# A second level of Strassen for product 4 of the output (g22 by w_out's fourth sum), with its quarters in attention's PSUM banks

## The chip, the cores and the metric

The kernel runs on one core of one Trainium2 chip. The metric is the device time of the whole kernel in microseconds (us), inputs and outputs in the chip's memory; lower is better. All data are float32.

The engines are named as the profile names them: PE (TensorE, matrix products), PEld (its loading of weights, beside the products), DVE (VectorE), ACT (ScalarE), POOL (GpSimd) and SP (SyncE, which here issues most transfers). TensorE writes its results to PSUM, [...] and VectorE and ScalarE empty them.

## The reference

```python
# attention without softmax, per batch b (8) and head h (8), seq 576, head_dim 64
kv  = np.einsum('bhsd,bhse->bhde', k, v)
out = np.einsum('bhsd,bhde->bhse', q, kv)
rms = np.sqrt(np.mean(out * out, axis=-1, keepdims=True) + 1e-06)
out = out / rms * g_norm
# then two layers on 4608 tokens of 512: w_in is 512 x 2048, w_out 2048 x 512
x = out.transpose(0, 2, 1, 3).reshape(4608, 512)
h = x @ w_in
g = np.maximum(0.01 * h, h)
return g @ w_out
```

Nearly all of the work is in the two large products, x @ w_in and g @ w_out.

## The kernel before

The 4608 tokens are worked in nine blocks of 512 (i = 0 to 8). The hidden units are worked in four groups (c = 0 to 3). A pair (block, group), from block 1 on, is a round, numbered n = (i - 1) * 4 + c, 0 to 31. Block 0 is computed without Strassen, at the start.

**Products by Strassen.** Each large product of a round is split into 2 x 2 quarters and computed as seven products of quarters rather than eight (the Winograd form). The products are numbered 1 to 7. Products 1, 6, 7 and 4 accumulate one after the other in one PSUM bank, products 2 or 5 and 3 in another; after each, the bank's running sum is added to the quarters of the output that need it:

```python
def strassen(tags, left, right, done, order=ORDER, pieces=None):
    banks = {}
    for i in order:
        if i is None:
            yield
            continue
        b = tags[0 if i in (1, 6, 7, 4) else 1]
        if i in FRESH:                              # FRESH = (1, 2, 5)
            banks[b] = ps_m.tile([P, 2, N2], F32, tag=b, name=f"{b[0]}_{b[1]}")
        bank = banks[b]
        ...
        for part in range(2):
            for r in range(2):                      # four matmuls of 128 x 256
                matmul(bank[:, part, :], lhsT=left(i, part, r), rhs=right(i, part, r),
                       start=i in FRESH and part == 0 and r == 0, stop=(r == 1), ...)
        done(i, bank.rearrange("p u (v n) -> p (u v) n", v=2))
        yield
```

**The hidden product (h), by two levels.** From block 2 on, each of the seven products of x @ w_in is again computed by seven, all as matmuls of 128 x 128. A round has seven h groups, in the order 1, 2, 6, 5, 7, 3, 4. Each h group has seven such matmuls and, where `second` is set, an eighth: it fills the fourth quarter of bank h_hb or h_hd with a matmul of product 2 of the output of an earlier round (g12 by w_out), which is by two levels too. The sums that make g from the seven, and the leaky ReLU, follow the seventh group:

```python
def product_h_two(i, c, quarters, to, second):
    ...
    for t, k in enumerate(ORDER):                   # ORDER = (1, 2, 6, 5, 7, 3, 4)
        for js, tags, q in zip(GROUPS, (("ha", "hc"), ("hb", "hd")), (qa, qc)):
            ...                                     # four matmuls in ha or hc, three in hb or hd
            if len(js) < 4 and second:
                second.product(k, banks[tag][:, 3, :])
            ...
            if fresh:
                nc.scalar.copy(q[:, at], bank)
            else:
                add(nc.vector, q[:, at], bank, q[:, at])
            if len(js) < 4 and second:
                second.done(k, banks[tag][:, 3, :])   # a 128 x 128 add into the output
        read(n0 + t + 1 + RING)                     # w_in's next operand, from memory
        yield
    g11, g21, g22, g12 = g_of(c)
    add(nc.vector, g21, qa[:, :, 0, :], qa[:, :, 1, :])
    add(nc.vector, g11, qa[:, :, 0, :], qc[:, :, 0, :])
    yield
    ...                                             # five more sums
    for t in (g11, g12, g22, g21):
        relu(t)                                     # ScalarE
    sums_of(c, to)                                  # GpSimd: the sums of g that Strassen needs
```

**The output product (o).** It follows two slots behind h. A slot holds one h group and then one o group; a round has seven slots. In rounds n = 4 to 29 product 2 is left to the h groups, and the order of the o groups is 1, 5, 6, none, 7, 3, 4. The banks are oa and oc; from one round to the next they change places:

```python
def product_o(n, g_sides, os, finish, second):
    w_sides, _ = sides_w2(n)
    sums = sides_w2(n + 1)[1] if n + 1 < NC * (NB - 1) else lambda i: None
    ...
    into = {1: ("11", True), 5: ("22", True), 2: ("11", False), 6: ("12", True),
            3: ("12", False), 7: ("22", False), 4: ("21", True)}

    def done(i, bank):
        key, fresh = into[i]
        ...
        if c == 0 and fresh:
            nc.scalar.copy(to, bank)
        else:
            add(nc.vector, to, bank, to)            # 128 x 512
        ...
        if i == (6 if second else 5):
            sums(0)                                 # the next round's sums of w_out, t12
        elif i == 4:
            sums(1)                                 # and t34: from memory, on SyncE's queue

    yield from strassen((("oa", "oc"), ("oc", "oa"))[n % 2], ...,
                        (1, 5, 6, None, 7, 3, 4) if second else ORDER, pieces=pieces)
```

**Attention** for the next block runs beside these, in pieces, at fixed slots (`FINE_SLOTS`, `LATE_SLOTS`). It has two PSUM banks of its own; the other six are ha, hb, hc, hd, oa and oc:

```python
ps_att = ctx.enter_context(tc.tile_pool(name="ps_att", bufs=2, space=PSUM))   # tag "att"
ps_m   = ctx.enter_context(tc.tile_pool(name="ps_m", bufs=1, space=PSUM))
...
FINE_SLOTS = {1: 1, 2: 1, 4: 1, 9: 1, 10: 2, 11: 1, 12: 1, 15: 1, 16: 2, 17: 2, 18: 1, 19: 1,
              23: 1, 24: 1, 25: 1, 26: 1}           # slot in the block (7 * c + t): steps
HELD = (22, 24, 26)                                 # slots without an o group in the last block

def both_outputs(b, lo, hi, sums, kv=None):
    tiles = att_tiles("o_ps")                       # both banks
    ...                                             # matmuls 64 x 32, then:
    for l in range(2):
        nc.scalar.activation(sq, o_ps[l], func=AF.Square)
    for l in range(2):
        for e in range(2):
            nc.scalar.activation(x[:, 2 * l + e, :], o_ps[l][:, e, :], func=AF.Copy, ...)
```

A slot's order, with what it emits: the h group; the attention's steps of this slot, x's sums for the next block (VectorE at slots 20 to 22, GpSimd at 24 and 25) and the transfers; `inner_g` (four GpSimd sums of g for product 2's second level, two at the fifth slot of a round and two at the seventh); at last the o group. From block 2 on each engine works in the order in which the program emits.

Of the kernel before, what the change touches and what calls it, by code (L numbers as in the profile page):

```python
# [23 lines left out]
def kernel(  # L24
# [39 lines left out]
    P = 128  # L64
# [34 lines left out]
    NW = U * NE * P  # L99
    w1_all = consts.tile([P, 2 * NC * NW], F32, name="w1_all")  # L100
    stage = consts.tile([P, 3 * NW], F32, name="stage")
    pairs = consts.tile([P, 4 * NW], F32, name="pairs")
    g_all = [consts.tile([P, 4 * U * N2], F32, name=f"g_{i}") for i in range(2)]

    def view(t, lo, *shape):
        n = 1
        for d in shape:
            n *= d
        t = t[:, lo:lo + n]
        names = "abcd"[:len(shape)]  # L110
        return t.rearrange(f"p ({' '.join(names)}) -> p {' '.join(names)}",
                           **dict(zip(names, shape))) if len(shape) > 1 else t

    def pair(i, *shape):
        return view(pairs, i * NW, *shape)

    def matmul(*args, **kw):
        pin(nc.tensor.matmul(*args, **kw))  # L118
# [66 lines left out]
    zeros = view(g_all[0], 0, NT)  # L185
    nc.vector.memset(zeros[:, :64], 0.0)
    nc.vector.memset(zeros[:, 64:], 0.0)
    ident = consts.tile([P, P], F32, name="ident")

    def make_ident():  # L190
        pin(nc.gpsimd.memset(ident, 1.0))
# [449 lines left out]
    def sides_w1(c):  # L641
# [9 lines left out]
        def more():  # L651
# [5 lines left out]

    w2_dram = [[dram.tile([P, 2, U, N2], F32, name=f"w2_{c}_{i}") for i in range(2)]
               for c in range(NC)]
    t12, t34 = pair(2, 2, U, N2), pair(3, 2, U, N2)  # L660
    writes = []

    def sides_w2(n):

        c = n % NC
        b11, b12 = w2_sb[0][c][:, :, :N2], w2_sb[0][c][:, :, N2:]
        b21, b22 = w2_sb[1][c][:, :, :N2], w2_sb[1][c][:, :, N2:]

        def sums(i):
            t = (t12, t34)[i]
            if n >= NC:
                pin(nc.sync.dma_start(t, w2_dram[c][i]))
                return
            if i == 0:
                add(nc.gpsimd, t[:, 0], b12, b11, True)
                add(nc.gpsimd, t[:, 1], b22, t[:, 0], True)
            else:
                add(nc.gpsimd, t[:, 0], b22, b12, True)  # L680
                add(nc.gpsimd, t[:, 1], b21, t12[:, 1], True)
            if (n, i) == (NC - 1, 1):

                writes.append((w2_dram[c][i], t))
            else:
                pin(nc.sync.dma_start(w2_dram[c][i], t))
        return {1: b11, 2: b21, 3: b22, 5: t12[:, 0], 6: t12[:, 1], 7: t34[:, 0],
                4: t34[:, 1]}, sums
# [49 lines left out]
    def read(to):  # L738
        nonlocal n_read
        while n_read < min(to, len(reads)):  # L740
# [5 lines left out]
    qc = pair(0, 4, 3, P)  # L746
    xt1 = [work.tile([P, 2, N2], F32, tag="xt1", name="xt1"),
           view(w1_all, RING * NG + 24 * P, 2, N2)]
    xt24 = [work.tile([P, 2, 2, N2], F32, tag="xt24", name="xt24"),
            view(w1_all, RING * NG + 16 * P, 2, 2, N2)]  # L750
    xi = view(stage, 0, 3, 7, P)

# [82 lines left out]
    def g_of(c):  # L835


        return [view(g_all[c % 2], 0, 4, 4, P)[:, :, i, :] for i in range(4)]
# [40 lines left out]

    gi = view(pairs, 12 * P, 4, P)

    def inner_w2(c):
        y = w2_sb[1][c]
# [7 lines left out]

    def inner_g(c, half):

        g = g_of(c)[3]
        a11, a21, a12, a22 = (g[:, n, :] for n in range(4))
        s1, s2, s3, s4 = (gi[:, n, :] for n in range(4))
        if half == 0:
            add(nc.gpsimd, s1, a21, a22)  # L900
            add(nc.gpsimd, s2, s1, a11, True)
        else:
            add(nc.gpsimd, s3, a11, a21, True)
            add(nc.gpsimd, s4, a12, s2, True)

    class Second:
# [17 lines left out]
        def done(self, k, bank):  # L924
            v, s = INTO[k]
            to = self.o[:, v, s * P:s * P + P]
            add(nc.vector, to, bank, to)
            if self.n % NC == NC - 1 and k == ORDER[-1]:
                self.finish("11", self.o)

    def product_h_two(i, c, quarters, to, second):

# [41 lines left out]
    def product_o(n, g_sides, os, finish, second):  # L974

        c = n % NC
        w_sides, _ = sides_w2(n)
        sums = sides_w2(n + 1)[1] if n + 1 < NC * (NB - 1) else lambda i: None
        if c == 0:

            for key in ("12", "22", "11", "21"):
                os[key] = opool.tile([P, 2, N2], F32, tag="o", name=f"o{key}", bufs=6)


        pieces = ((0, slice(0, N2)), (1, slice(0, P)), (1, slice(P, N2))) \
            if n + 1 == NC * (NB - 1) else None
# [5 lines that stand above are left out]
            if isinstance(bank, list):  # L992
                for at, (end, (part, cols)) in enumerate(zip(bank, pieces)):
                    to = os[key][:, part, cols]
                    add(nc.vector, to, end, to)
                    if i == ORDER[-1]:
                        finish(key, os[key], part, cols, (nc.sync, nc.scalar)[at % 2])
                if i == 7:
                    finish(key, os[key])
                return  # L1000
            to = os[key].rearrange("p u (v n) -> p (u v) n", v=2)
# [3 lines that stand above are left out]
                add(nc.vector, to, bank, to)  # L1005
            if c == NC - 1 and i in (2, 7, 3, 4):
                finish(key, os[key])

            if i == (6 if second else 5):
                sums(0)  # L1010
            elif i == 4:
                sums(1)


        yield from strassen((("oa", "oc"), ("oc", "oa"))[n % 2], lambda i, part, r: g_sides[i][:, 2 * r + part, :],
                            lambda i, part, r: w_sides[i][:, r, :], done,
                           (1, 5, 6, None, 7, 3, 4) if second else ORDER,
                           pieces=pieces)
# [100 lines left out]
    HELD = (22, 24, 26)  # L1119
    o_queue, waited = collections.deque(), 0  # L1120

    seconds = {}

    def second_of(n):
        if n in seconds:
# [9 lines left out]
    for i in range(1, NB):  # L1135
# [4 lines left out]
        for c in range(NC):  # L1140
# [3 lines left out]
            for t in range(7):  # L1144
                slot = 7 * c + t
                go(h_steps, 1)
                if not one:

                    if t == 6:
                        go(h_steps, 1)  # L1150
                    if slot in LATE_SLOTS:
                        go(late, 1)
                    for _ in range(FINE_SLOTS.get(slot, 0)):
                        go(a_steps, 1)
                    if i + 1 < NB:
                        if slot == 20:
                            x_sides, new_quarters, sums, inner = sides_x(i + 1)
                        if slot in (20, 21, 22):
                            go(sums, 2 if slot == 20 else 1)
                        if slot == 24:  # L1160
                            inner(0)
                        elif slot == 25:
                            inner(1)
                    load_some()

                now = (i - 1) * NC + c
                if now - 1 in seconds:
                    for half in range(2):
                        if t == (6 if half else 4):
                            inner_g((now - 1) % NC, half)  # L1170
                    if t == 5 and now <= 2 * NC:
                        inner_w2((now - 1) % NC)
                if slot == 4 and not one:
                    while writes:
                        pin(nc.sync.dma_start(*writes.pop()))
                if slot in HELD and i == NB - 1:
                    pass
                elif waited == LAG:
                    go_o()
                elif o_queue:  # L1180
                    waited += 1
                if one:

                    if t == 1:
                        combine(c, 2)
                    if t == 3 and c < NC - 1:
                        h_sides, more_h = sides_w1(c + 1)
                        combine(c + 1, 0)
                    if t == 5 and c < NC - 1:
                        more_h()  # L1190
                        combine(c + 1, 1)
                    if slot == 5:
                        in_line = True
                        go(late, 1)
                        in_line = False
                    if slot in A_SLOTS:
                        go(a_steps, 1)
                    load_some()
                    if slot == 24:
                        go(a_steps)  # L1200
                        x_sides, new_quarters, sums, inner = sides_x(i + 1)
                        go(sums)
                    elif slot == 25:
                        inner(0)
                    elif slot == 26:
                        inner(1)
# [47 lines left out]
```

## Time and profile before

| | |
|---|---|
| time, median of 3 runs | 918.29 us (917.94 to 919.58) |
| span of the profiled run | 916.1 us |
| PE busy | 909.3 us, 99% |
| DVE busy | 631.6 us, 69% |
| POOL busy | 370.2 us, 40% |
| ACT busy | 328.2 us, 36% |
| moved by DMA | 200.05 MB, mean 218 GB/s |
| 128 x 512 add of a bank of oc into the output, DVE | 684 ns |
| 128 x 128 add of the fourth quarter of hb into the output, DVE | 287 ns |
| 128 x 128 sum of g, POOL | 459 ns |

The profile comes from one execution. The page gives busy times by engine, then groups of instructions with count and mean time of one; other views give the waits by engine, and all instructions in order of time. In these lines out<-in are the names of the tiles written and read, L118 is the line of the helper through which all matmuls go, and L637 the one of the helper for additions and subtractions. A float32 matmul is recorded as two instructions. The lengths of matmuls are modelled and overlap; the time that one takes up is read from where the next one starts.

### The profile page before, as it was taken

The page shows a single profiled execution, that of the slowest core. Times are in us where ns is not written, and L with a number is a line of the kernel's source. Part 1 is how long each engine was busy: PE and PEld are TensorE (multiplying, and loading weights), DVE is VectorE, ACT ScalarE, POOL GpSimd, SP SyncE. Part 2 cuts the span into 40 slices and gives each one's busy share as a digit, 9 for nine tenths or more (in the row PEclk, how much of TensorE's full clock was granted, in tenths as well). Part 3 has the DMA queues.
Part 4 walks back from the last instruction along what each step waited for, and adds up shares of the span by engine and source line. Part 5 has one row for each costly group of instructions (what it writes and reads, how often), then busy time and mean ns, then how long its engine had stood idle before and what let it go on. Part 6 is the DMA issues. An engine that isn't in the chain of part 4 may idle for free.

```text
span 916.1 us, 18037 instructions
## 1 busy us (share of the span) xinstructions
PE 909.3 (99%) x6980; PEld 776.3 (85%) x6980; DVE 631.6 (69%) x1168; ACT 328.2 (36%) x645; POOL 370.2 (40%) x438
## 2 busy tenths in 40 slices
PE   9999999999999999999999999999999999999998
PEld 5444448888998999899999999999999999999997
DVE  4876995587457876587756786678659755755565
ACT  5454533242135233533343324332343333223330
POOL 2000355967633473226421642264226422642222
DMA  8999926885599778776886789658765676667632
GB/s 269 236 245 249 248 85 191 280 285 167 166 360 289 228 209 268 233 230 214 255 247 230 219 249 272 222 178 212 242 183 176 187 222 198 185 185 223 197 109 92
DMA packets 90228, 200.05 MB, mean 218 GB/s; under 512 B 9888, under 2 KB 42272, under 8 KB 90144
## 3 DMA queue, kind: packets, MB, share of 16 engines
q1 hardware_dynamic: 79680, 187.04, 68.6%
q10 hardware_dynamic: 10016, 10.69, 3.4%
q8 instruction: 55, 0.90, 0.4%
q0 software_dynamic: 448, 1.18, 0.3%
q14 instruction: 29, 0.24, 0.1%
HBM read 172.39 MB, written 26.48 MB: 217 GB/s over the span
## 4 chain that ended last, share of the span: by engine, by line
PE 96%; DMA 2%; DVE 1%; issue 0%; ACT 0%; POOL 0%; SPq 0%; ACTq 0%; DVEq 0%; POOLq 0%
PE o_a L118 19%; PE o_c L118 18%; PE h_ha L118 11%; PE h_hb L118 11%; PE h_hc L118 8%; PE h_hd L118 8%; PE o_acc L118 6%; PE h_ps L118 6%; PE o_ps L118 3%; PE h_a L118 2%; PE h_b L118 1%; PE h_c L118 1%; PE h_d L118 1%; PE kv_ps L118 1%; DMA pairs<-in_v_dram 1%; DMA v_in<-in_v_dram 1%
## 5 line engine op out<-in xcount | busy, mean ns | idle before, releaser
L637 POOL TENSOR_TENSOR gs<-g 128x512 f32<-128x512 f32 x64 | 81.7, 1277 | 253.3 <-ACT g L833 253.3
L833 ACT ACTIVATE g<-g 128x512 f32<-128x512 f32 x124 | 78.2, 631 | 131.9 <-DVE g L637 131.9
L952 ACT COPY w_all<-h_ha 128x512 f32<-128x512 f32 x84 | 48.9, 582 | 173.5 <-PE h_ha L118 167.8
L118 PE MATMUL o_a<-pairs,gs 128*128 128x256 f32 x384 | 91.3, 381 | 0.0
L118 PE MATMUL o_c<-pairs,gs 128*128 128x256 f32 x376 | 89.2, 380 | 0.0
L637 DVE TENSOR_TENSOR o<-h_hb,o 128x128 f32<-128x128 f32 x104 | 29.8, 287 | 83.8 <-ACT pairs L952 83.7
L637 DVE TENSOR_TENSOR o<-o_c,o 128x512 f32<-128x512 f32 (+1 forms) x91 | 61.2, 672 | 23.9 <-PE o_c L118 23.6
L118 PEld LDWEIGHTS o_a<-pairs,gs 128*128 128x128 f32 x384 | 69.8, 190 | 9.2 <-POOL pairs L637 1.2
L118 PEld LDWEIGHTS o_c<-pairs,gs 128*128 128x128 f32 x376 | 68.3, 190 | 7.6
L637 DVE TENSOR_TENSOR o<-o_a,o 128x512 f32<-128x512 f32 x75 | 51.2, 683 | 28.2 <-PE o_a L118 28.1
L637 POOL TENSOR_TENSOR pairs<-w_all 128x512 f32<-128x512 f32 x8 | 11.1, 1384 | 120.6 <-ACT cut L245 102.3
L118 PE MATMUL h_ha<-stage,w_all 128*128 128x128 f32 x448 | 59.6, 276 | 0.0
L118 PEld LDWEIGHTS h_ha<-stage,w_all 128*128 128x128 f32 x448 | 56.6, 192 | 3.0 <-issue 0.7
L118 PE MATMUL h_ps<-xT,w_all 128*128 128x512 f32 (+1 forms) x136 | 58.0, 570 | 0.9 <-DVE w_all L258 0.9
L118 PE MATMUL o_acc<-w,g 128*128 128x512 f32 x128 | 57.8, 595 | 0.0
L637 DVE TENSOR_TENSOR g<-g,pairs 128x512 f32<-128x512 f32 x84 | 55.7, 689 | 1.9
L637 POOL TENSOR_TENSOR pairs<-g 128x128 f32<-128x128 f32 x52 | 23.9, 459 | 75.4 <-PE h_hb L118 46.7
L118 PEld LDWEIGHTS h_ps<-xT,w_all 128*128 128x128 f32 x136 | 25.5, 190 | 30.0 <-issue 26.6
L637 DVE TENSOR_TENSOR w_all<-h_hc,w_all 128x512 f32<-128x512 f32 x56 | 38.3, 684 | 15.9 <-PE h_hc L118 15.8
L118 PEld LDWEIGHTS o_acc<-w,g 128*128 128x128 f32 x128 | 24.0, 190 | 29.8 <-issue 29.4
L637 DVE TENSOR_TENSOR o<-h_hd,o 128x128 f32<-128x128 f32 x78 | 22.1, 283 | 37.8 <-ACT pairs L952 37.7
L118 PE MATMUL h_hb<-stage,w_all 128*128 128x128 f32 x336 | 46.7, 275 | 0.0
(228 smaller groups left out, 2264.6 us busy)
## 6 DMA issues: line engine op xcount, KB each, us to landing
w_all<-w SPq DMA_DIRECT2D x196, 448.0 KB, 4.2
pairs<-w SPq DMA_DIRECT2D x56, 512.0 KB, 4.3
out_dram<-o ACTq DMA_DIRECT2D x35, 256.0 KB, 4.6
v_in<-in_v_dram SPq DMA_DIRECT2D x29, 288.0 KB, 5.7
k_in<-in_k_dram SPq DMA_DIRECT2D x28, 288.0 KB, 5.1
q_in<-in_q_dram SPq DMA_DIRECT2D x56, 144.0 KB, 6.0
q_in<-in_q_dram SPq DMA_DIRECT2D x56, 140.0 KB, 5.8
w<-stage SPq DMA_DIRECT2D x12, 512.0 KB, 4.6
```

What stands on the lines that cost most here:

```text
L118: pin(nc.tensor.matmul(*args, **kw))
L637: ins = eng.tensor_tensor(out_, a, b_, op=ALU.subtract if minus else ALU.add)
L833: nc.scalar.activation(t, t if src is None else src, func=AF.Prelu, alpha=SLOPE)
L952: nc.scalar.copy(q[:, at], bank)
```

## The change

Product 4 of the output multiplies g22 by a sum of w_out's quarters. In rounds n = 8 to 29 (blocks 3 to 8) it is no longer four matmuls of 128 x 256 but, by a second level of Strassen, seven of 128 x 128 (quarter products, here q1 to q7). This needs:

- seven operands from w_out (`f4` and `f4_more`): GpSimd makes the three sums and the fourth once per group (`inner_w4`, rounds 4 to 7), they are written to memory, and each later round reads them back;
- four sums of g22: `inner_g` makes them together with those for product 2, 128 x 256 in place of 128 x 128;
- two banks: those of attention. q1, q6, q7 and q4 accumulate in one, q2 and then q5 and q3 in the other. They stand between the groups of the output product: q1 and q2 in the slot that had no o group, q6 and q5 before o7, q7 and q3 after it, q4 in the slot that had o3; o3 moves into the slot that had o4;
- seven additions of 128 x 128 into g21's part of the output, in place of one of 128 x 512. And since product 4 no longer accumulates on products 1, 6 and 7, their running sum is added to that part by an addition of its own (`third`).

The identity matrix moves into a tile that is used later for x's sums, which makes room for the second set of g's sums. Cut to its core:

```diff
+    f4 = t34[:, 1].rearrange("p u (v n) -> p (u v) n", v=2)
+    f4_more = view(stage, 21 * P, 3, P)
+    def four(n):
+        return 2 * NC <= n < NC * (NB - 1) - 2
...
+            if four(n) and i:
+                pin(nc.sync.dma_start(t[:, 0], w2_dram[c][i][:, 0]))
+                pin(nc.sync.dma_start(f4, w4_dram[c][:, :4, :]))
+                pin(nc.sync.dma_start(f4_more, w4_dram[c][:, 4:, :]))
+                return
...
-        g = g_of(c)[3]
-        a11, a21, a12, a22 = (g[:, n, :] for n in range(4))
-        s1, s2, s3, s4 = (gi[:, n, :] for n in range(4))
+        g = view(g_all[c % 2], 0, 4, 4, P)
+        a11, a21, a12, a22 = (g[:, n, 2:, :] for n in range(4))
+        s1, s2, s3, s4 = (gi_two[:, :, n * P:n * P + P] for n in range(4))
...
+    class Fourth:
+        BEFORE = {3: (1, 2), 4: (6, 5), 5: (4,)}
+        AFTER = {4: (7, 3)}
+        ...
+        def some(self, which):
+            for k in which:
+                if k == 1:
+                    self.banks = [ps_att.tile([P, P], F32, tag="att", name="f_ps")
+                                  for _ in range(2)]
+                bank = self.banks[0 if k in (1, 6, 7, 4) else 1]
+                matmul(bank, lhsT=self.left[k], rhs=self.right[k], start=k in FRESH, stop=True,
+                       skip_group_check=True)
+                v, s = INTO[k]
+                to = self.os["21"][:, v, s * P:s * P + P]
+                if self.n % NC == 0 and k in (1, 6, 5):
+                    nc.scalar.copy(to, bank)
+                else:
+                    add(nc.vector, to, bank, to)
+        def third(self, bank):
+            to = self.os["21"].rearrange("p u (v n) -> p (u v) n", v=2)
+            if self.n % NC:
+                add(nc.vector, to, bank, to)
+                return
+            nc.scalar.copy(to[:, 2, :], bank[:, 2, :])
+            add(nc.vector, to[:, :2, :], bank[:, :2, :], to[:, :2, :])
+            add(nc.vector, to[:, 3, :], bank[:, 3, :], to[:, 3, :])
+        def beside(self, steps, last):
+            for j in range(7):
+                self.some(self.BEFORE.get(j, ()))
+                if j == 5:
+                    last()                          # sums(1): the next round's operands
+                next(steps)
+                self.some(self.AFTER.get(j, ()))
+                yield
...
+            if fourth and i == 7:
+                fourth.third(bank)
...
+        if four(n):
+            fourth = Fourth(n, os)
+            yield from fourth.beside(strassen(..., (1, 5, 6, None, 7, None, 3)), last)
+            return
```

## The prediction

> **What bounds the kernel now.** I read the busy times first, then the waits, then the chain that ended last.
>
> ```profile
> PE 909.3 (99%) x6980; PEld 776.3 (85%) x6980; DVE 631.6 (69%) x1168; ACT 328.2 (36%) x645; POOL 370.2 (40%) x438
> ...
> PE 96%; DMA 2%; DVE 1%; issue 0%; ACT 0%; POOL 0%; SPq 0%; ACTq 0%; DVEq 0%; POOLq 0%
> ```
>
> TensorE is busy 99% of the span, and 96% of the chain that ended last is TensorE. The list of waits has four entries for it, 3.4 us in all, none of them in the seven blocks that use the hidden product by two levels. So every microsecond of matmuls saved is a microsecond won, and every microsecond that TensorE is made to wait is lost in full. VectorE has 31% free on average, but it works in order, and its work comes in bursts. I therefore looked at one round (from the last h group of hidden group c = 0 in block 8 to the next round) in order of time, TensorE first:
>
> ```profile
> 823.27 1.06 PE L118 MATMUL h_ha<-stage,w_all 128*128 128x128 f32 x8
> ...
> 825.06 1.89 PE L118 MATMUL o_c<-pairs,gs 128*128 128x256 f32 x8
> 826.79 0.39 PE L118 MATMUL h_ha<-xT,w_all 128*128 128x128 f32 x2
> ...
> 828.57 1.89 PE L118 MATMUL o_a<-w,gs 128*128 128x256 f32 x8
> 830.30 0.38 PE L118 MATMUL h_hc<-xT,w_all 128*128 128x128 f32 x2
> ...
> 832.09 1.89 PE L118 MATMUL o_c<-pairs,g 128*128 128x256 f32 x8
> 833.82 1.05 PE L118 MATMUL h_ha<-stage,w_all 128*128 128x128 f32 x8
> ...
> 835.60 1.03 PE L118 MATMUL o_a<-w,g 128*128 128x256 f32 x4
> ```
>
> Columns: start, length, engine, line, operation, out<-in, count. An fp32 matmul is two instructions, so x8 on h_ha is four matmuls. The groups, named by product: h4 from 823.27, o7 from 825.06, h1 from 826.79, o3 from 828.57, h2 from 830.30, o4 from 832.09, h6 from 833.82, the next round's o1 from 835.60. An h group takes 1.78 us (8 matmuls of 0.223), an o group 1.73. VectorE in the same stretch:
>
> ```profile
> 826.02 0.68 DVE L637 TENSOR_TENSOR g<-w_all 128x512 f32<-128x512 f32 x1
> 826.62 0.68 DVE L637 TENSOR_TENSOR g<-w_all,pairs 128x512 f32<-128x512 f32 x1
> 827.23 0.68 DVE L637 TENSOR_TENSOR o<-o_c,o 128x512 f32<-128x512 f32 x1
> 827.83 1.48 DVE L637 TENSOR_TENSOR g<-g,w_all 128x512 f32<-128x512 f32 x2
> 829.34 2.02 DVE L637 TENSOR_TENSOR g<-g,pairs 128x512 f32<-128x512 f32 x3
> 832.42 0.29 DVE L637 TENSOR_TENSOR o<-h_hb,o 128x128 f32<-128x128 f32 x1 [1.06 <-ACT pairs L952]
> 832.63 0.68 DVE L637 TENSOR_TENSOR o<-o_a,o 128x512 f32<-128x512 f32 x1
> 833.23 0.68 DVE L637 TENSOR_TENSOR w_all<-h_hc,w_all 128x512 f32<-128x512 f32 x1
> ...
> 834.29 0.28 DVE L637 TENSOR_TENSOR o<-h_hd,o 128x128 f32<-128x128 f32 x1
> ```
>
> Seen here: the two g sums start 2.75 us after h4 does. Back to back, VectorE starts a 128x512 add every 0.60 us and a 128x128 one every 0.20 (the lengths, 0.68 and 0.29, overlap). The o3 add, done about 833.31, is 2.3 us ahead of o1 at 835.60. That is the slack that the change spends.
>
> [...] o3 (o_a), o4 (o_c), o1 (o_a) rotate and TensorE never waits. [...] the rows have 287 and 684, so four quarters of an add take 1.7 times as long as the whole. [...] the 128x512 subtraction xT<-xT takes 1.29 us at 502.78, beside GpSimd's sums, where one takes 0.68 at 496.05.
>
> **The change, part by part.** It concerns 22 output products, n = 8 to 29.
> 1. *Matmuls.* o4 (1.73 us) becomes seven 128x128 matmuls, 7 x 0.223 = 1.56. Saved: 22 x 0.17 = 3.8 us. This is all there is to gain.
> 2. *VectorE and ScalarE.* Seven 128x128 additions and one more 128x512 one (product 7's running sum also goes to g21's output) replace one 128x512: 7 x 0.20 to 0.29 more, some 2 us a round of 24 us, 44 us in all. The average bears that (69% to about 74%); the bursts may not.
> 3. *GpSimd and transfers.* The g sums of 128x128 (0.46 us) become 128x256 (0.73), four a round; 192 KB more a round, 4.2 MB in all beside 200. GpSimd waits most of the time, the operands are asked for four slots ahead and land after 4.3 us: I count nothing.
> 4. *Order.* In the changed program, as built, TensorE's order is h4, q6, q5, o7, q7, q3, h1, q4, h2, o3, h6, next o1 (q: the quarter products). Two things follow. q7 and q3 reuse the two attention banks of q6 and q5 after one o group. And o3 now stands where o4 stood: the next o1 takes the bank that o3 has just left, with one h group between them instead of two h groups and an o4.
>
> *The wait at q7 and q3.* VectorE's order is: g sum, g sum, q6, q5, o7, o7 again, q7, q3, five more g sums. From h4's start: q6 is added from 2.75 + 1.20 = 3.95, and q5 is through at 4.44. TensorE has h4, q6, q5, o7 done at 1.785 + 0.445 + 1.73 = 3.96, would have q3 start at 4.18 and may at about 4.50: **0.31 us** lost. In the rounds with n a multiple of 4 ScalarE empties q6 and q5, and nothing is lost.
>
> *The wait at o1.* The five g sums start at 6.2 instead of 4.56 (q6, q5, o7 again, q7, q3: 0.2+0.2+0.6+0.2+0.2, and 0.2 for dependences): 1.64 later. With them the ReLUs, ScalarE's copy of h_hb, which stands behind the ReLUs, and the add behind that copy move by 1.64. Then stand, before the o3 add and no longer behind it, q4 (0.20), h_hc (0.60), h_hd (0.46) and one of 128x128 (0.20). The o3 add ends at 833.31 - 823.27 = 10.04, + 1.64 + 1.46 = 13.14. TensorE reaches o1 at 12.33 (835.60 - 823.27) - 1.73 (o4) + 5 x 0.223 (q6, q5, q7, q3, q4; q1 and q2 come before h4) = 11.71, + 0.31 = 12.02. Lost: **1.17 us**. Where ScalarE takes part, the sums start at 5.85 and 1.13 is lost.
>
> By kind of round:
> - n = 11, 15, 19, 23, 27: 0.31 + 1.17 = 1.48; five, 7.4 us.
> - n = 9, 13, 17, 21, 25: x's sums for the next block lie in this burst: two between the g sums and q6 (496.05 to 497.38 in the trace, 1.25 us), a third before q4 (1.2, beside GpSimd), a fourth before o3 (1.1). At q3 1.56; o3's add ends at 13.14 + 3.5 = 16.6, TensorE is there at 13.3: 3.3. Five of 4.9, 24.5; n = 29 has no x's sums and held slots, 0.3.
> - n = 10, 14, 18: the two g sums start 0.6 later (ScalarE's spread copies, 423.63 in the trace), and a transpose of qT (pitch 1.1) stands before o3: 0.91 + 2.2 = 3.1, three, 9.3; n = 22 and 26 without the transpose 2.1 and 1.5.
> - n = 8, 12, 16, 20, 24, 28: 1.13, six, 6.8. In the first four the attention's o_ps, in both banks, is emitted right before q1 and q2, and these wait until ScalarE has read it:
>
> ```profile
> 369.22 1.09 PE L118 MATMUL o_ps<-qT,kv 64*32 64x256 f32 x32
> ...
> 370.24 1.16 PE L118 MATMUL h_ha<-stage,w_all 128*128 128x128 f32 x8
> 370.42 1.09 ACT L416 ACTIVATE sq<-o_ps 128x512 f32<-128x512 f32 x2 [2.29 <-PE o_ps L118]
> ...
> 371.39 1.57 ACT L421 ACTIVATE xT<-o_ps,g_sb 128x256 f32<-128x256 f32 x4
> ```
>
>   TensorE would go on at 370.24; the copies end at 372.96, so q2 starts 2.6 us late. For the narrower pieces of the next three blocks the same reading gives 2.15, 1.75 and 1.3. Sum 7.8.
>
> Lost: 7.4 + 24.8 + 12.9 + 6.8 + 7.8 = 59.7 us. Won: 3.8. Net **+56**: 974. Part of these delays may fall together or hide in one another, so I take 970.
>
> **Rivals.** (a) *The saving holds*: the burst drains faster than I think, all waits vanish, 914.5. For it: VectorE is idle 31%, and the tuned kernel had no such wait. Against it: the order of instructions is fixed in the program, and the slack of 2.3 us is smaller than the 3.1 us that the o3 add moves plus 0.3 by which o1 comes earlier. (b) *Only the attention's banks hurt*: +7.8 - 3.8, 922. For it: this wait is certain, four times. Against: as for (a). (c) *Operands late*: w_out's 704 KB land behind the queue's other transfers, or GpSimd's 128x256 sums come too late for q7. Each microsecond in 22 rounds is 22 us: 990 or more. Against: four slots are 14 us, and GpSimd's four sums at 420.30 would end by 423.2 where q7 begins at 424.3. (d) *VectorE becomes the bound*: some 19 of 24 us are used in a round; not on average.
>
> **Range and chances.** The steps read from single rows are good to about 0.3 us a round, 7 us in all; whether VectorE stands beside GpSimd (5 x 2 us) and how far waits overlap makes up the rest. Range 948 to 988. Slower by over 2% needs +18.4 us, a third of the sum: 0.93. Within 2% (rival b, or a): 0.06. Faster by over 2% can't come out of a saving of 3.8 us: 0.01.
>
> **What would show it.** TensorE's waits: on VectorE at the first matmul of o1 (o_a and o_c from w_out and g) about 22 times, some 40 us in all; at f_ps on VectorE some 15; at f_ps on ScalarE four times, 7 to 8. TensorE's busy share falls to about 94%. No wait of TensorE on GpSimd or on a transfer. The prediction is wrong if the o1 wait is missing or under 0.5 us in the rounds n = 11, 15, 19, or if a wait on a transfer is among the first three.

## The result, and the profile after

The changed kernel takes 981.1 us (median; 977.1 to 988.8) against 918.4 us: ratio 1.069, 95% interval 1.065 to 1.073. The prediction was 970, range 948 to 988.

Busy times and the chain that ended last, from the page of the changed kernel (L638 is now the line of the helper for additions):

```profile
PE 922.7 (94%) x7112; PEld 781.4 (80%) x7112; DVE 670.3 (68%) x1316; ACT 331.3 (34%) x663; POOL 405.1 (41%) x454
...
PE 65%; DVE 22%; ACT 4%; DMA 4%; issue 2%; POOL 2%; SPq 0%; DVEq 0%; ACTq 0%; POOLq 0%
```

Before, 96% of that chain was TensorE; now 22% of it is VectorE, although VectorE's share of busy time went from 69% to 68%. The average shows nothing; the chain shows that TensorE stands behind single additions. TensorE's waits (what waited, for what: us in total, times, longest):

```profile
PE o_a L118 <- DVE o L638: 12.8, 10, 3.3
PE o_c L118 <- DVE o L638: 12.1, 11, 1.8
PE f_ps L118 <- DVE o L638: 10.8, 16, 1.6
PE f_ps L118 <- ACT xT L422: 6.2, 5, 2.0
PE o_c L118 <- DMA pairs<-w: 3.1, 1, 3.1
...
PE h_hb L118 <- DVE o L638: 1.1, 1, 1.1
```

The first two entries are o1 (o_a or o_c by turns, since the banks change places), 21 times. The third is q7 and q3, the fourth q1 and q2 behind attention (two entries in n = 8, one each in n = 12, 16 and 20). The fifth is a transfer, at n = 7. One plain round (n = 27); TensorE, its waits in brackets:

```profile
861.73 0.46 PE L118 MATMUL f_ps<-stage,pairs 128*128 128x128 f32 x2 [0.26 <-DVE o L638]
...
866.04 1.89 PE L118 MATMUL o_c<-w,gs 128*128 128x256 f32 x8
...
870.41 1.99 PE L118 MATMUL o_c<-w,g 128*128 128x256 f32 x8 [0.69 <-DVE o L638]
```

and VectorE in order of time:

```profile
860.09 0.68 DVE L638 TENSOR_TENSOR g<-w_all 128x512 f32<-128x512 f32 x1
860.69 0.69 DVE L638 TENSOR_TENSOR g<-w_all,pairs 128x512 f32<-128x512 f32 x1
861.29 0.48 DVE L638 TENSOR_TENSOR o<-f_ps,o 128x128 f32<-128x128 f32 x2
861.69 1.28 DVE L638 TENSOR_TENSOR o<-o_a,o 128x512 f32<-128x512 f32 x2
863.08 0.49 DVE L638 TENSOR_TENSOR o<-f_ps,o 128x128 f32<-128x128 f32 x2
863.49 1.41 DVE L638 TENSOR_TENSOR g<-g,w_all 128x512 f32<-128x512 f32 x2
864.93 2.02 DVE L638 TENSOR_TENSOR g<-g,pairs 128x512 f32<-128x512 f32 x3
...
869.48 0.28 DVE L638 TENSOR_TENSOR o<-h_hd,o 128x128 f32<-128x128 f32 x1
869.68 0.68 DVE L638 TENSOR_TENSOR o<-o_c,o 128x512 f32<-128x512 f32 x1
```

o3 (o_c, 866.04) is through on TensorE at 867.8, but its addition runs from 869.68 to 870.36, last in VectorE's row, and o1, which takes the same bank o_c, starts at 870.41. Before, 2.3 us lay between these two. An entry is shorter than the loss, since the end of a matmul is modelled and covers part of each wait: by the starts of the groups this round loses 0.49 us at q7 and q3 (0.42 of it at q7) and 0.96 at o1, where 0.26 and 0.69 are shown.

Laying o1's start after against before, round by round, gives what each round lost, net of any saving:

| rounds | predicted, net, each | measured, us |
|---|---|---|
| n = 11, 15, 19, 23, 27 | 1.31 | 1.30, 1.29, 1.29, 1.28, 1.29 |
| 9, 13, 17, 21, 25 | 4.73 | 3.29, 3.19, 3.08, 4.17, 4.98 |
| 10, 14, 18 | 2.93 | 2.23, 2.31, 2.44 |
| 22; 26 | 1.93; 1.33 | 1.49; 2.68 (1.7 of a lower clock) |
| 8, 12, 16, 20 | 3.56, 3.11, 2.71, 2.26 | 5.56 (1.7 of a lower clock), 3.58, 3.18, 2.77 |
| 24, 28 | 0.96 | 1.47, 1.47 |
| 29 | 0.13 | 1.96 |
| sum, n = 8 to 29 | 55.9 | 56.3 |
| all else | 0 | 6.1 (2.8 before round 0, 3.3 at n = 7) |

What is lost before round 0 is not a steady cost of the change: in the traces of the eleven experiments below that start from the changed kernel it lies between -0.5 and 9.7 us (to o1 of n = 1), though the program is the same there. The three largest, 7.3 to 9.7, come with waits for v's transfer of 5.5 to 6.8 us.

One execution of the move of o3 alone, an experiment below, had a granted clock of 0.85 throughout (1046.7 us), and neither its time nor its waits are used.

### The profile page after: what moved, and what is told of

Read it like the earlier page. It is cut to its first block, busy times and chain, and to the rows that moved or that the text cites. A ratio compares the mean times of both kernels' runs of the same rounds, so it can differ in the third digit from the quotient of the medians.

```text
span 979.1 us, 18597 instructions
## 1 busy us (share of the span) xinstructions
PE 922.7 (94%) x7112; PEld 781.4 (80%) x7112; DVE 670.3 (68%) x1316; ACT 331.3 (34%) x663; POOL 405.1 (41%) x454
## 3 DMA queue, kind: packets, MB, share of 16 engines
HBM read 176.72 MB, written 28.31 MB: 209 GB/s over the span
## 4 chain that ended last, share of the span: by engine, by line
PE 65%; DVE 22%; ACT 4%; DMA 4%; issue 2%; POOL 2%; SPq 0%; DVEq 0%; ACTq 0%; POOLq 0%
PE o_a L118 13%; PE o_c L118 11%; DVE g L638 10%; DVE o L638 7%; PE h_ha L118 6%; PE h_hb L118 6%; PE h_hc L118 5%; PE h_hd L118 5%; PE o_acc L118 5%; PE h_ps L118 5%; PE o_ps L118 2%; DVE w_all L638 2%; ACT pairs L1023 2%; ACT g L846 1%; DMA v_in<-in_v_dram 1%
## 5 line engine op out<-in xcount | busy, mean ns | idle before, releaser
L638 POOL TENSOR_TENSOR gs<-g 128x512 f32<-128x512 f32 x64 | 81.7, 1277 | 292.3 <-ACT g L846 292.3
L638 DVE TENSOR_TENSOR o<-o_c,o 128x512 f32<-128x512 f32 (+1 forms) x91 | 60.4, 674 | 34.6 <-PE o_c L118 34.4
L638 DVE TENSOR_TENSOR o<-o_a,o 128x512 f32<-128x512 f32 (+2 forms) x87 | 54.7, 640 | 36.7 <-PE o_a L118 34.1
L638 DVE TENSOR_TENSOR o<-h_hb,o 128x128 f32<-128x128 f32 x104 | 29.8, 287 | 66.9 <-ACT pairs L1023 66.9
L638 POOL TENSOR_TENSOR pairs<-g 128x256 f32<-128x256 f32 x52 | 38.4, 739 | 59.7 <-PE h_hb L118 39.9
L638 POOL TENSOR_TENSOR pairs<-w_all 128x512 f32<-128x512 f32 x8 | 11.1, 1387 | 124.2 <-DMA stage<-in_moe_w_in_dram 94.4
L638 DVE TENSOR_TENSOR g<-g,pairs 128x512 f32<-128x512 f32 x84 | 56.1, 694 | 1.9
L638 DVE TENSOR_TENSOR o<-h_hd,o 128x128 f32<-128x128 f32 x78 | 22.2, 285 | 49.3 <-ACT pairs L1023 49.3
L118 PE MATMUL o_a<-w,g 128*128 128x256 f32 x152 | 38.6, 398 | 12.8 <-DVE o L638 12.8
L638 DVE TENSOR_TENSOR w_all<-h_hc,w_all 128x512 f32<-128x512 f32 x56 | 38.4, 685 | 15.8 <-PE h_hc L118 15.8
```

Source lines behind the costliest of these rows:

```text
L638: ins = eng.tensor_tensor(out_, a, b_, op=ALU.subtract if minus else ALU.add)
```

## The experiments

The theory: TensorE waits for single PSUM banks, because the order of the program puts their additions late. Rivals: VectorE has too much to do at these places in any order, so that a wait taken away comes back elsewhere; attention alone; preparation and transfers. Times are medians; the ratio is to the kernel before on the same chip, with its 95% interval.

**Other banks for o1.** The product tiles no longer change places.

```diff
+    def tags_of(n):
+        last = NC * (NB - 1) - 1
+        flip = n % 2 if n < 2 * NC else n == last
+        return (("oa", "oc"), ("oc", "oa"))[int(flip)]
...
-                strassen((("oa", "oc"), ("oc", "oa"))[n % 2],
+                strassen(tags_of(n),
```

> Edit: in rounds n = 8 to 30 the output product's two banks no longer change places from round to round, so the next o1 takes the bank of o7 (left four groups ago) and not that of o3 (left one h group ago). All work is kept. Theory (the wait is for one bank, not for VectorE's throughput): the waits at o1, some 20 of about 1 us, go; the waits at f_ps (q7, q3) stay; the wait for o3's bank now falls at the next o5, an o and an h group later, where it is over. 945 to 955 us. Rival (VectorE's bursts are too long in themselves, so the wait only moves to o5 or to an h group): 973 to 981, with waits on VectorE at o_c<-w or h groups of the same sum. Rival (preparation and transfers): unchanged, 981.

Measured: 952.3 us, ratio 1.036 (1.031 to 1.041). TensorE's longest waits, by cause:

```profile
PE f_ps L118 <- DVE o L638: 10.7, 16, 1.6
PE f_ps L118 <- ACT xT L422: 6.2, 5, 2.0
PE o_c L118 <- DMA pairs<-w: 4.4, 1, 4.4
```

Both o1 entries are gone and no new one over 0.4 us has come; f_ps stands as it was. The 28.8 us won are the 24.9 us of the two entries and 21 times the 0.2 that the records cover. No work was taken from VectorE: the bank was the cause.

**o3 back in its slot**, with all the rest of the change.

```diff
-                         (1, 5, 6, None, 7, None, 3)), last)
+                         (1, 5, 6, None, 7, 3, None)), last)
```

> Edit: in the changed rounds o3 stands again where it stood in the kernel before (slot 5, one slot earlier), with q4 ahead of it; the slot that o4 held stays without an output product. Banks, all products and all additions are those of the changed kernel. Theory (o1 waits for the bank of o3 because o3 was moved): the o3 add gains an h and a half groups' time, so the waits at o1 go in the plain rounds and shrink in the rounds with x's sums; the waits at f_ps stay: 947 to 958 us, near the 952.3 of the run that reassigned the banks. Rival (VectorE's throughput after all): 970 to 981.

Measured: 951.9 us, ratio 1.033 (1.030 to 1.037). A second, independent way to the same 29 us: the bank is free in time because o3 comes earlier.

**The move of o3 alone**, in the kernel before.

```diff
-                           (1, 5, 6, None, 7, 3, 4) if second else ORDER,
+                           (1, 5, 6, None, 7, 4, 3) if second else ORDER,
```

> Edit: the kernel before, with the last two output products of a round in the other order (o4, then o3): so o3 stands in the last slot, and the next o1 takes the bank that o3 has just left, as in the changed kernel, but with no quarter products and none of their additions. Theory (the move alone uses up the slack, and it is the quarter products' additions that push VectorE over it): in plain rounds the last addition ends at 835.1 where o1 starts at 835.60, so no wait; in the five rounds with x's sums it ends at 507.6 where o1 would start at 506.53, so 1.1 to 1.4 each: 922 to 930 us. Rival (the order of the banks alone costs it): 22 waits of about 1 us, 940 or more.

Measured: 938.3 us, ratio 1.021 (1.019 to 1.023). Both expectations missed. The trace of the kernel before tells why I was low: the last addition of a round ends after the start of the next o1 in eleven rounds: in the six with x's sums (n = 5, which this edit touches too, 9, 13, 17, 21, 25) by 1.0 to 2.9 us, and in the rounds behind them, n = 6, 10, 14, 18 by 1.1 to 1.25 and n = 22 by 0.2. That is 14.9 us, and some 17 with the 0.2 that each wait costs above what the records show. I had counted five. In the plain rounds at least 0.43 us of slack is left, which only the quarter products' additions use up. So the move costs about 20 us alone. Some 3.4 of the 17 fall to n = 5 and 6, rounds that the changed kernel leaves as they were; so of the 29 us I put 16 to 17 down to the move and 12 to 13 to the quarter products' additions. This split, and that the eleven rounds make up most of the 20, is an estimate from the trace of the kernel before, not seen in this run.

**Attention one slot earlier.**

```diff
-                    for _ in range(FINE_SLOTS.get(slot, 0)):
+                    for _ in range(FINE_SLOTS.get(slot, 0) if i < 3 or slot not in (11, 12)
+                                   else {11: 2, 12: 0}[slot]):
```

> Edit: in blocks 3 on, attention's step of slot 12 is done in slot 11, one slot earlier, so that ScalarE has an h and an o group's time to empty o_ps before q1 and q2 take its banks. All work is kept. Theory: the waits of f_ps on ScalarE (6.2 us shown in 5) go and little else changes: 972 to 975 us. Rival (attention's banks are the main cost): 922 to 930. Rival (VectorE's throughput): no gain, 979 to 983, since the late operand sums follow anyway.

Measured: 974.1 us, ratio 1.059 (1.052 to 1.066). The entry f_ps <- ACT is gone. Rounds 12, 16 and 20 lose 1.46, 1.47, 1.48 in place of 3.58, 3.18, 2.77, what rounds 24 and 28 lose without attention. At n = 8 a transfer came to light behind it (3.5 us). The time is where the theory put it; the executions range from 969 to 980 us, so the rounds are the better proof.

**q7, q3 and q4 later.**

```diff
-        BEFORE = {3: (1, 2), 4: (6, 5), 5: (4,)}
-        AFTER = {4: (7, 3)}
+        BEFORE = {3: (1, 2), 4: (6, 5), 5: (7, 3), 6: (4,)}
+        AFTER = {}
...
-                if j == 5:
+                if j == 6:
                     last()
```

The next round's operands (`last`) are asked for one slot later too.

> Edit: q7 and q3 stand one slot later (beside h2's slot rather than right after o7), and q4 one slot later than that, before h6, with product 3's and 4's order otherwise kept. All work is kept. Theory: the waits of f_ps on VectorE (10.8 us shown in 16) go; o1 still waits for o3's bank, and since q7, q3 leave the burst ahead of the g sums but q4's add moves nearer to o3's, the o1 waits change by less than 0.4 us a round either way: 964 to 974 us. Rival (VectorE's throughput): what is taken from f_ps comes back at o1, 979 to 983.

Measured: 1028.9 us, ratio 1.119 (1.115 to 1.123): wrong for both, by 46 us and more. TensorE's first entry, and one of its 21 waits:

```profile
PE f_ps L118 <- DVE o L638: 65.5, 21, 5.0
```

```profile
908.61 0.49 PE L118 MATMUL f_ps<-pairs,g 128*128 128x128 f32 x2 [2.47 <-DVE o L638]
```

VectorE ahead of it:

```profile
903.54 1.41 DVE L638 TENSOR_TENSOR g<-g,w_all 128x512 f32<-128x512 f32 x2
904.98 2.02 DVE L638 TENSOR_TENSOR g<-g,pairs 128x512 f32<-128x512 f32 x3
908.06 0.29 DVE L638 TENSOR_TENSOR o<-h_hb,o 128x128 f32<-128x128 f32 x1 [1.06 <-ACT pairs L1023]
908.27 0.48 DVE L638 TENSOR_TENSOR o<-f_ps,o 128x128 f32<-128x128 f32 x2
```

I had moved q7's matmul past the place where the program emits the five g sums. Its addition fell behind them, and q4, in the same bank, waits for it. It is the same mechanism, made worse by a step that looked like relief.

**The preparation alone**: product 4 is done whole, no quarter products.

```diff
     def four(n):
-        return 2 * NC <= n < NC * (NB - 1) - 2
+        return False
```

> Edit: product 4 is done whole in all rounds as before the change; kept are the preparation (the second level's sums of w_out's fourth sum on GpSimd, their writes to DRAM, the moved tile of the identity) and the wider sums of g22. Theory: the preparation costs only what stands at single places (2.8 us in the first two blocks, and perhaps 3 at n = 7): 920 to 925 us. Rival (preparation, wider sums or transfers hold TensorE back all through): 940 or more.

Measured: 924.5 us, ratio 1.006 (1.004 to 1.008). In its trace no round from n = 8 on loses or wins more than 0.1 us; 2.2 us are lost at n = 7 to the transfer. So the preparation, its writes and the wider g sums cost 5 us of the 63, more than the 3.8 that the matmuls were to save. The profiled execution is the fastest of all (920.4), so its trace does not show where the rest of the 5 lies. And this version does not read the seven operands back (172.39 MB read from memory, as before the change; 176.72 in the changed kernel), so it leaves the cost of these reads open. In the traces with quarter products no round from n = 9 on has a wait of TensorE for a transfer; at n = 8 there is one of 2.2 to 4.2 us in six of them.

**x's sums elsewhere** (slots 23 and 24).

```diff
-                        if slot in (20, 21, 22):
-                            go(sums, 2 if slot == 20 else 1)
+                        if slot in (23, 24):
+                            go(sums, 2)
```

> Edit: only the four x sums for the next block (on VectorE, slots 20, 21 and 22 of a block) are moved to slots 23 and 24. All work is kept, also the banks that change places. Theory (a wait costs where a burst of VectorE falls together with it): the five rounds n = 9, 13, 17, 21, 25 lose 3.3, 3.2, 3.1, 4.2 and 5.0 us and would then lose 1.3 as the plain ones: 981.1 - 12, and a little more where the clock stays up: 966 to 971 us. Rival (VectorE's throughput): the sums cost the same where they now stand, 978 to 983.

Measured: 995.2 us, ratio 1.083 (1.078 to 1.088). The five rounds did as the theory said, and more: four of them lose 0.44, the fifth 1.0. But the rounds behind them, n = 10, 14, 18 and 22, lose 8.2 to 8.5 each, and n = 26 4.6. TensorE at n = 10:

```profile
437.91 1.22 PE L118 MATMUL f_ps<-stage,pairs 128*128 128x128 f32 x4 [3.96 <-POOL pairs L638]
```

GpSimd there:

```profile
427.21 1.04 POOL L638 TENSOR_TENSOR stage<-xT 128x256 f32<-128x256 f32 x1 [4.93 <-DVE xT L638]
...
435.88 1.17 POOL L638 TENSOR_TENSOR pairs<-g 128x256 f32<-128x256 f32 x1
437.13 0.72 POOL L638 TENSOR_TENSOR pairs<-pairs,g 128x256 f32<-128x256 f32 x1
```

GpSimd's own x sums stand first in its row and waited 4.93 us for VectorE's; the g sums for q6 and q5 queue behind. Both expectations missed, and "VectorE has no room" was not the reason: the third engine in line was.

**q6 and q5 added ahead of the g sums.** In blocks 3 on VectorE adds them before the first two g sums, and before the x sums of slot 20 (`held_back` runs behind q6 and q5).

```diff
                 self.some(self.BEFORE.get(j, ()))
+                while j == 4 and held_back:
+                    held_back.pop(0)()
...
-                    if t == 6:
+                    if t == 6 and i < 3:
                         go(h_steps, 1)
+                    elif t == 6:
+                        held_back.append(lambda: go(h_steps, 1))
...
+                            if slot == 20 and i > 2:
+                                held_back.append(lambda: go(sums, 2))
```

> Edit: in blocks 3 on VectorE does the additions of q6 and q5 ahead of the first two g sums of the round, and ahead of the two x sums of slot 20, instead of behind them. TensorE's order, banks and all work are those of the changed kernel. Theory (q7 and q3 wait because the additions of q6 and q5 stand behind those sums in VectorE's order): the waits of f_ps on VectorE (10.7 us shown in 16) go; the sums can't start before h4 is added, so they are hardly later, and the o1 waits stay as they are or grow by up to 0.4 us a round, since TensorE comes to o1 earlier and VectorE does not: 966 to 976 us. Rival (VectorE's throughput): all of the gain comes back at o1, 979 to 983.

Measured: 986.5 us, ratio 1.073 (1.069 to 1.077). The waits:

```profile
PE o_a L118 <- DVE o L638: 14.0, 10, 3.5
PE o_c L118 <- DVE o L638: 13.1, 11, 2.0
PE o_c L118 <- DMA pairs<-w: 5.2, 1, 5.2
PE f_ps L118 <- DVE o L638: 4.8, 5, 1.1
```

Eleven of the 16 waits of q7 and q3 are gone, and nothing is won: plain rounds still lose 1.28 to 1.30 (n = 19 2.93, under a lower clock), and the rounds with x's sums 3.07 to 4.98. TensorE comes to o1 earlier and waits there longer, since VectorE's addition of o3 is no earlier. Behind this later wait for the same engine, the earlier one cost nothing. Here the rival was right about the place, though 986.5 lies above its range. (The 5 us more than in the changed kernel lie at n = 7, 12 and 19: the transfer, and a lower clock behind waits.)

**All three together**: o3 back, attention in slots 9 and 10, q6 and q5 ahead of the sums.

> Edits: the three that the theory names together: o3 stands where it stood before, attention's steps of slots 11 and 12 are done in slots 9 and 10, and the additions of q6 and q5 stand ahead of the g and x sums. All work is kept. Theory: 951.9 - 6.2 - 5 x 0.2 (attention) - 10.7 - 16 x 0.2 (q7, q3) = 931, range 926 to 937; what is left above the kernel before are a transfer at n = 7 or 8 and the preparation. Rival (VectorE's throughput): the waits come back at o1 or at an h group, 944 or more.

Measured: 944.2 us, ratio 1.026 (1.023 to 1.029): above the theory's range, where the rival begins. With o1 free, the same edit of q6 and q5 now wins 0.2 us a plain round (0.12 lost against 0.33 with o3 back alone). The five rounds with x's sums keep their 1.77 (2.17 once), the wait now at q4, 4.8 us in 5. In this profile, 30.6 us longer than the one before the change, 9.7 were lost before round 0 (waits for v's transfer of 6.8, and 3.4 of a lower clock), 6.2 at n = 7 and 8 and 9.2 in the five rounds.

What holds a plain round for its last 0.12 us is the bank h_hb. TensorE and VectorE at the end of n = 27:

```profile
862.94 0.94 PE L118 MATMUL h_hb<-stage,w_all 128*128 128x128 f32 x6
```

```profile
859.51 2.02 DVE L638 TENSOR_TENSOR g<-g,pairs 128x512 f32<-128x512 f32 x3
862.59 0.29 DVE L638 TENSOR_TENSOR o<-h_hb,o 128x128 f32<-128x128 f32 x1 [1.06 <-ACT pairs L1025]
```

h6 comes to h_hb 0.19 us late (1.08 us after h_ha, which started at 861.86, in place of 0.89), right behind VectorE's addition of the bank's fourth quarter, which ends at 862.88. VectorE had been idle for 1.06 us ahead of it, waiting for ScalarE: ScalarE's copy out of the same bank (862.10 to 862.56) stands behind its ReLUs, and these stand behind the g sums. The kernel before has the same idle 1.06 us, ahead of 832.42 in the prediction's lines.

**The two x sums of slot 20 behind that slot's additions**, in addition.

```diff
                             if slot == 20 and i > 2:
+                                pass
...
                 while held_back:
                     held_back.pop(0)()
+                if slot == 20 and 2 < i < NB - 1:
+                    go(sums, 2)
```

> Edits: those of e10, and the two x sums of slot 20 stand behind all of that slot's additions, so that q4's bank, which q7 leaves, doesn't stand behind them. Theory: the five waits of f_ps that are left (4.8 us shown, 1.77 a round with the 0.2 hidden) go, down to 0.1 to 0.3 a round: 944.2 - 7.5 = 934 to 939 us. Rival (VectorE has no room for the sums there either): the same time as e10, with the wait at o1 or at an h group.

Measured: 948.0 us (937.7 to 949.6), ratio 1.029 (1.021 to 1.036). The five rounds lose 1.76 to 2.17 as before, to another entry:

```profile
PE h_hb L118 <- DVE o L638: 5.3, 5, 1.1
```

One of the five, n = 13, TensorE and then VectorE:

```profile
523.42 0.94 PE L118 MATMUL h_hb<-stage,w_all 128*128 128x128 f32 x6 [1.05 <-DVE o L638]
```

```profile
523.08 0.29 DVE L638 TENSOR_TENSOR o<-h_hb,o 128x128 f32<-128x128 f32 x1 [1.06 <-ACT pairs L1025]
```

Three places for one wait (q7, q4, an h group) and the same 1.77 us, some 9 us in five rounds: in all three orders the two x sums stand ahead of the five g sums. As a forecast the rival was right. But VectorE's throughput alone is not the cause: VectorE works nearly without a gap from 513.63 to 522.01, and then stands idle for 1.06 us while TensorE waits for it, since ScalarE's copy out of h_hb is behind the ReLUs. And with the x sums in slots 23 and 24 (in the run above) the five rounds lost 0.44 to 1.0. Whether ScalarE's copy ahead of the ReLUs would free the round was not tried.

**q1, q2, q6 and q5 earlier**, with the banks of the first experiment and attention in slots 9 and 10.

```diff
-        BEFORE = {3: (1, 2), 4: (6, 5), 5: (4,)}
-        AFTER = {4: (7, 3)}
+        BEFORE = {3: (6, 5), 5: (4,)}
+        AFTER = {2: (1, 2), 4: (7, 3)}
```

> Edits: the banks do not change places (as in e1), attention's steps of slots 11 and 12 are done in slots 9 and 10, q1 and q2 stand after o6 and q6 and q5 one slot earlier (ahead of h4), so that VectorE has their additions behind it before the two g sums; q7, q3, q4 stay. All work is kept. Theory: the waits of f_ps on VectorE (10.7 us shown in 16, with 0.2 hidden in each) and on ScalarE (6.2 us) go: 952.3 - 14 - 7.5 = 929 to 936 us. Rival (VectorE's bursts are too long in themselves): the wait comes back at q4 or at an h group, 944 or more.

Measured: 955.2 us, ratio 1.039 (1.035 to 1.043), no better than the banks alone, and above the theory's range; the number is the rival's, but neither named the place where most of the wait came. TensorE's first two waits:

```profile
PE f_ps L118 <- POOL pairs L638: 7.8, 5, 2.2
PE f_ps L118 <- DVE o L638: 6.3, 6, 1.5
```

q6 and q5 now ask for their sums of g a slot before GpSimd has them, in five rounds, and the rounds with x's sums stay at 1.6 to 1.8.

**And product 7's operand loaded at once** in rounds 4 to 7, which the change had put behind the preparation.

```diff
             elif i == 4 and NC <= n < 2 * NC:
                 inner_w4()
+                sums(1, 0)
                 later.extend(([1, lambda: (
...
-                    [2, lambda: sums(1)]))
+                    [2, lambda: sums(1, 1)]))
```

`sums(1, 0)` loads the first half of the tile, with product 7's operand, `sums(1, 1)` the second.

> Edits: those of e6, and in the four rounds in which the operand of product 7 was loaded late (with the other half of its tile, behind the preparation), that half is loaded at once as in the kernel before. Theory: the wait of TensorE for a transfer at n = 7 (3.1 to 4.4 us shown, and about 1.7 of a lower clock behind it) goes: e6 minus 3 to 6, 924 to 931 us. Rival (the transfer is late for want of bandwidth and not because it was asked for late): same as e6.

Measured: 952.7 us, ratio 1.038 (1.032 to 1.043), not told apart from the version without it. In its trace round 7 loses 0.01 where it lost 5.98, and round 8 loses 6.63 where it lost 2.97, for f_ps behind a transfer of 4.2. The wait moved by one round, and the time is the rival's. Whether that queue is short of bandwidth there was not tried.

## Why the prediction was right, point by point

- **Bank of o3, the wait at o1: right.** Predicted 1.17 in plain rounds with 0.31 at q3, in sum 1.48; measured 0.96 and 0.49, net of the saving 1.29 for 1.31. (The prediction's sum, 13.14 less 12.02, gives 1.12; for the other 0.05 it shows no line.) Two edits that free the bank in different ways give back the same 29 us. "Some 40 us in all" was too high: 24.9 are shown, 29 were lost.
- **q7 and q3: the place right, the worth not.** Some 15 waits were predicted and 16 came. The sum of 1.48 was right because I took the 0.31 off o1's wait again; as a separate cost it does not exist while o1 waits. And 0.49 for 0.31 with 0.96 for 1.17 is one error, met twice with opposite signs.
- **x's sums: mis-sized**, 4.9 predicted, 3.1 to 3.3 plus the 0.17 saved in n = 9, 13, 17. I had TensorE reach o1 as in a plain round. In these rounds attention's matmuls lie between h6 and o1 and hide part: 2.2 to 2.4 us of them in n = 9, 13 and 17, where 1.1 to 1.4 us of wait are shown, 1.3 in n = 21 (2.23 shown), none in n = 25 (3.35 shown), where 4.98 came, net.
- **n = 10, 14, 18: somewhat high**, 2.93 for 2.2 to 2.4.
- **ScalarE's rounds: mis-sized**, 0.96 for 1.47. I left out that `third` waits in VectorE's row for ScalarE's copy of one quarter, which is 0.33 of the missing 0.51 (n = 28):

```profile
910.85 0.62 DVE L638 TENSOR_TENSOR o<-o_a,o 128x256 f32<-128x256 f32 x2 [0.33 <-ACT o L989]
```

- **Attention's banks: right.** 2.6, 2.15, 1.75 and 1.3 predicted; above the 1.47 of such a round 2.4 (n = 8, less 1.7 for the clock), 2.1, 1.7 and 1.3 measured, and gone when attention goes earlier.
- **n = 29: missed.** h_hb waits 1.05 us for VectorE there; I had 0.3.
- **VectorE's work: right**, 44 us more predicted, 38.7 measured (670.3 - 631.6), and its throughput was no bound over the 22 rounds; the five rounds with x's sums keep 1.77 us each in the three orders tried, with ScalarE's copy in the chain.
- **"I count nothing" for GpSimd and transfers: wrong by 5 us**, in the preparation with its writes. "No wait on a transfer" failed at n = 7 (3.1 us), and at n = 8 once attention's wait was gone.
- **The saving of 0.17 a round was never seen.** With no wait listed in a plain round of the three edits together, the round still loses 0.12; its h6 group takes 2.07 us there where 1.78 is usual, held by h_hb, as shown above. That bank stood in no line of the prediction as one that TensorE waits for.

In the 22 rounds the terms that were too high (x's sums 4.9 us, n = 10, 14 and 18 1.8, n = 22 0.4) and those too low (ScalarE's rounds 4.5, with 1.7 of lower clock in n = 8; n = 26 1.35, by its clock; n = 29 1.8) cancel: the sum of 56 is better than its parts, by luck. The 4 us that I took off for delays that hide in one another did not come, and 6.1 lie outside the 22 rounds: that is why 981 was measured for 970. No version tried beats the kernel before. The best with quarter products, 944.2 us, still carries the preparation, the transfers at n = 7 and 8, and the 9 us of the five rounds, against at most 3.8 to win.

## What to carry to other kernels

Before a product is moved in a kernel whose engines work in program order, look which bank the next product takes and where in the emptying engine's row the addition of that bank then stands: slack in the row (2.3 us here), not the engine's average (VectorE 69% busy), pays for it. Look too whether that row waits for another engine there: here VectorE stood idle for 1.06 us a round ahead of an addition that TensorE needed. Of a chain of waits for one engine only the last counted here (eleven waits of q7 and q3 taken away, and the plain rounds still lost 1.28 to 1.30 us), so mend from the end of the round backwards, and look after each mending which engine's row the moved work now heads. A saving of 0.4% in matmuls is worth the trial only if its preparation costs less than that.

## What the runs showed of the hardware

Some waits cost TensorE more than their length. The changed kernel at 844.76 us has waited 3.35 us for VectorE; around that its clock, us by us (start:end, length, busy of PE, PEld, DVE, ACT and POOL, then the granted clock, DMA share, GB/s):

```profile
843.00:844.00 1.00, 0.00 (x0) 0.00 (x0) 1.00 (x1) 0.00 (x0) 1.00 (x2) 1.00 0.82 333
844.00:845.00 1.00, 0.24 (x1) 0.24 (x2) 0.91 (x3) 0.00 (x0) 1.00 (x1) 0.70 0.06 25
845.00:846.00 1.00, 1.00 (x3) 0.82 (x4) 0.00 (x0) 0.00 (x0) 0.23 (x1) 0.50 0.00 0
846.00:847.00 1.00, 1.00 (x3) 0.79 (x3) 0.00 (x0) 0.00 (x0) 0.00 (x0) 0.50 0.00 0
847.00:848.00 1.00, 1.00 (x4) 0.80 (x3) 0.00 (x0) 0.00 (x0) 0.00 (x0) 0.59 0.00 0
848.00:849.00 1.00, 1.00 (x11) 0.97 (x10) 0.69 (x1) 0.00 (x0) 0.00 (x1) 1.00 0.00 0
```

Half the clock for 3.4 us (in steps of 0.4 us 0.51 at 844.4, 0.50 from 844.8 to 847.6, 0.73 at 847.6, 1.00 from 848.0), 0.30 + 0.50 + 0.50 + 0.41 = 1.7 us lost, while from 845 on matmuls run without a gap. A dip of the version with q4 late has the same length and depth (0.67, 0.50, 0.50, 0.62 from 476 to 480 us, 1.71 lost). Not every wait was followed by one: in the profiles of the changed kernel and eleven of the experiments, between 300 and 940 us, such a dip (a stretch of 2 us under 0.9 within 10 us) followed 1 of 99 waits of 0.7 to 1.5 us, 9 of 40 of 1.5 to 2, 12 of 26 of 2 to 3, and 19 of 21 longer ones. What decides it for a single wait was not shown. The version with q4 late lost 34 us to a lower clock in its trace, the changed kernel 3.4 (two dips), the kernel before none. It is also part of the spread: the changed kernel ranges over 12 us, with a mean granted clock of 0.991 to 0.996 (0.005 of 980 us is 5), the one before over 3, with 1.00 in its profile.
